# Where the first rounding of the attention output stands on ScalarE and VectorE, and which weight conversions stand behind it

## Chip, core and metric

The kernel runs on one core of one Trainium2 chip. The metric is the device time of one execution in microseconds (us). TensorE is called PE below, VectorE DVE, ScalarE ACT, GpSimd POOL, and SyncE, whose queue issues most transfers, SP.

## What is computed

An attention with a local window and block summaries feeds two gated or leaky feed-forward layers. Cut to what matters:

```python
k_sum = k.reshape(B, H, nb, 32, D).max(axis=3)      # 2 x 8 heads, 768 positions, D = 64
v_sum = v.reshape(B, H, nb, 32, D).mean(axis=3)
scores = concat([where(|i - j| < 16, q @ k.T / 8, -1e9), q @ k_sum.T / 8 + log(32)])
x = softmax(scores) @ concat([v, v_sum])            # 1536 tokens x 512
y = ((x @ w_a) * (x @ w_b)) @ w_out                 # 512 -> 1536 -> 512
h = y @ w_in; out = maximum(0.01 * h, h) @ w_out2   # 512 -> 2048 -> 512
```

## The kernel before

The attention is worked off in pairs of (head pair, 256 positions). For each pair PE turns q, multiplies the scores (line 670, `ps_t<-kts,qt`), DVE adds the mask and finds the extreme (line 684), ACT takes the exponential (line 690), DVE normalizes it (lines 699 to 701, in `normal`), PE turns the result (line 711), ACT copies it (line 715) and PE multiplies it with the values (line 725, in `pv`). Four such pairs give the first 512 tokens of x, one 128-row slice `x_0` to `x_3` for each pair.

The feed-forward products run in three passes of float32r matmuls: each operand is split into a rounded high part and a remainder. For x this is done at the end of `pv`: ACT rounds (line 735), DVE subtracts (line 736). A product is high x high, high x low, low x high (`mm3`).

The weights are stored as 64-bit words and are converted piece by piece (`convert`): SP loads a piece of 512 KB into `wst` (three buffers); DVE takes the low word (line 388), ACT the high word (line 394, `wc<-wst`), DVE clamps (400), shifts (403) and joins (409), ACT rounds the high part into `wsp` (416) and DVE subtracts the low part (419). `wc` has two buffers, so a third piece's line 394 waits until the first piece's line 419 is done. The pieces come in the order a0, b0, a1, b1, a2, ... While the attention runs, the first four weights a0, b0, a1, b1 are multiplied with each slice of x as it appears, into four banks `ps_a`, `ps_b`, `ps_c` (two of these).

A list of operations with planned places (`ops`) is sorted and recorded; `tick(2)` puts two steps of conversion behind most products. A scheduler then decides the order on each engine; `tc.issue_after(x)` keeps what is inside behind x. `line` is a chain that the first pairs' DVE work follows (`behind`).

The values for later pairs lie in two tiles, `vw0` (`vw_99`) and `vw1` (`vw_100`), with the block means added by a copy on POOL (line 224, `put_sums`). The second batch's block sums are made by loading a quarter of the values with SP (line 176, into `vb0` = `vb_101`) and adding the other three quarters by accumulating transfers that POOL issues (line 178), each of which waits until the one before has landed. Each SP transfer uses one of eight completion semaphores in turn and waits for the transfer eight places ahead of it.

Of the kernel before, what the change touches and what calls it, by code (L numbers as in the profile page):

```python
# [21 lines left out]
def kernel(  # L22
# [12 lines left out]
    nc = tc.nc  # L35
# [54 lines left out]
    cnt = {"at": 0, "q": 0, "conv": 0, "st": 0, "load": 0, "credit": 0.0, "bg": 0.0}  # L90
    late = {}

    def at_bank():
        cnt["at"] += 1
        return bank(at_banks[cnt["at"] % len(at_banks)])
# [12 lines left out]
    def runs(p):  # L108

        (b, hp, g), y = p  # L110
        if y == (b, hp, g + 1):
            return [(0, b, hp, g, 2)]
        return [(j, *x, 1) for j, x in enumerate(p)]
# [19 lines left out]
    bg, vb_done = [], [None, None]  # L133

    pace = {"micro": 0.0, "bg": 3, "after": None}
# [95 lines left out]
    LOAD, SIDE, PRODUCT = range(3)  # L231
    PER = 8
    PV = 13
# [111 lines left out]
    def need(key):  # L345
        return 2 if key[0] == "s" else 1

    def by_dma(key):
        return key[0] == "o" and key[1] >= M1 or key[0] == "p" and key[1] < M2
# [4 lines left out]
    def stage():  # L354
        key = loads[cnt["st"]]
        cnt["st"] += 1
        nm, f = key
        t = wst_p.tile([P, 1024], I32, tag="wst", name="wst")
        if nm in "op":
            src = {"o": w_o, "p": w_o2}[nm][P * f : P * (f + 1), :]  # L360
            nc.sync.dma_start(out=t, in_=src)
        else:
            src = {"a": w_a, "b": w_b, "i": w_i}[nm][:, 2 * P * f : 2 * P * (f + 1)]
            nc.sync.dma_start(
                out=t.rearrange("p (k f) -> p k f", k=KT),
                in_=src.rearrange("(k p) f -> p k f", p=P),
            )
        staged[key] = t

    def convert():  # L370

        i = cnt["conv"]
        key = pieces[i]
        while cnt["st"] < min(load_no[key] + 3, len(loads)):
            stage()
        cnt["conv"] += 1
        assert room[0] >= need(key), key
        room[0] -= need(key)
        if key[0] == "s":
            combine(key)  # L380
            return
        ww = staged.pop(key).rearrange("p (f two) -> p f two", two=2)
        lo_w, hi_w = ww[:, :, 0], ww[:, :, 1]
        t = {}

        def low():
            t["r"] = wcv_p.tile([P, 512], I32, tag="wr", name="wr")
            nc.vector.tensor_scalar(
                out=t["r"], in0=lo_w.bitcast(U32), scalar1=2.0**-29, scalar2=7.0,
                op0=ALU.mult, op1=ALU.min,  # L390
            )
            t["c"] = wcv_p.tile([P, 512], I32, tag="wc", name="wc")
            with tc.issue_after(pace["turned"].ins):
                nc.scalar.activation(  # L394
                    out=t["c"].bitcast(F32), in_=hi_w.bitcast(F32), func=AF.Abs, scale=2.0**-112
                )

        def clamp():
            c = t["c"].bitcast(F32)
            nc.vector.tensor_scalar(out=c, in0=c, scalar1=F_MAX, scalar2=None, op0=ALU.min)  # L400

        def shift():
            nc.vector.scalar_tensor_tensor(  # L403
                out=t["c"], in0=t["c"], scalar=3, in1=t["r"],
                op0=ALU.logical_shift_left, op1=ALU.bitwise_or,
            )

        def join():
            nc.vector.scalar_tensor_tensor(  # L409
                out=t["c"], in0=hi_w, scalar=SIGN, in1=t["c"],  # L410
                op0=ALU.bitwise_and, op1=ALU.bitwise_or,
            )

        def high():
            t["w"] = wsp_p.tile([P, 2, 512], F32R, tag="wsp", name="wsp")
            t["high"] = nc.scalar.copy(out=t["w"][:, 0], in_=t["c"].bitcast(F32))  # L416

        def rest_of():
            nc.vector.tensor_tensor(  # L419
                out=t["w"][:, 1], in0=t["c"].bitcast(F32), in1=t["w"][:, 0].bitcast(F32),  # L420
                op=ALU.subtract,
            )
            w_of[key] = t["w"]
            kept[key] = t["c"].bitcast(F32)

        def negative():
            t["n"] = wcv_p.tile([P, 512], F32, tag="wr", name="neg")
            nc.scalar.activation(
                out=t["n"], in_=t["w"][:, 0].bitcast(F32), func=AF.Copy, scale=-1.0
            )  # L430
            nc.gpsimd.dma_start(out=t["n"], in_=t["c"].bitcast(F32), accum_op=ALU.add)

        def low_of(after=None):
            with tc.issue_after(after.ins) if after is not None else nullcontext():
                nc.scalar.copy(out=t["w"][:, 1], in_=t["n"])
            w_of[key] = t["w"]

        bg.extend([low, clamp, shift, join, high])
        if lag:
            lows = lag.pop()  # L440
            bg.append(lambda: lows(t["high"]))
        bg.append(negative if by_dma(key) else rest_of)
        if by_dma(key):
            lag.append(low_of)

    def combine(key):
        x, y = pairs_of[key]
        c = kept.pop(x), kept.pop(y)
        t = {}

        def sub(o, x, y, op=ALU.subtract):
            at = lambda z: c[z[0]][:, z[1] * HB : (z[1] + 1) * HB]
            nc.vector.tensor_tensor(out=at(o), in0=at(x), in1=at(y), op=op)

        def high(j):
            t[j] = wsp_p.tile([P, 2, 512], F32R, tag="wsp", name="wsp")
            nc.scalar.copy(out=t[j][:, 0], in_=c[j])

        def rest_of(j):
            nc.vector.tensor_tensor(  # L460
                out=t[j][:, 1], in0=c[j], in1=t[j][:, 0].bitcast(F32), op=ALU.subtract
            )
            if j == 0:
                w_of[key] = t

        bg.extend([
            lambda: sub((1, 1), (1, 0), (1, 1), ALU.add),
            lambda: sub((1, 0), (0, 0), (1, 0)),
            lambda: high(1),
            lambda: sub((0, 0), (1, 1), (0, 0)),  # L470
            lambda: sub((0, 1), (0, 1), (0, 0)),
            lambda: high(0),
            lambda: rest_of(1),
            lambda: rest_of(0),
        ])
# [161 lines left out]
    st, placed, line = {}, [], []  # L637

    def in_line(ins):
        line.append(ins.ins)  # L640

    def behind(on):
        return tc.issue_after(line[-1]) if on else nullcontext()
# [51 lines left out]

    def normal(i, j):
        pm, sm = st["pm", i, j]
        with behind(i == 0):
            nc.vector.tensor_scalar_add(sm, sm, 1.0e-9)
        nc.vector.reciprocal(out=sm, in_=sm)  # L700
        done = nc.vector.tensor_tensor(
            out=pm, in0=pm, in1=sm.unsqueeze(2).to_broadcast([P, G, P]), op=ALU.mult
        )
        if i < 2:
            in_line(done)
# [12 lines left out]
    def pv(i, p):  # L718
        vw = vw_of.pop(i)
        ps = at_bank()  # L720
        for j in range(2):
            pt = st.pop(("pt", i, j))
            for w in range(G):
                for c in range(2):
                    st["out"] = nc.tensor.matmul(  # L725
                        out=ps[c * D : (c + 1) * D, j * GT + w * W : j * GT + (w + 1) * W],
                        lhsT=vw[:, j * G + w, c, :],
                        rhs=pt[:, w, c * W : (c + 1) * W],
                        start=True, stop=True,
                    )  # L730
        for j, b, hp, g, n in runs(p):
            c, t0 = divmod(b * S + g * GT, T)
            src = ps[:, j * GT : (j + n) * GT]
            x = x_tile(c, hp)[:, :, t0 : t0 + n * GT]
            nc.scalar.copy(out=x[:, 0], in_=src)  # L735
            nc.vector.tensor_tensor(
                out=x[:, 1], in0=src, in1=x[:, 0].bitcast(F32), op=ALU.subtract
            )


    def mm3(ps, w, x, first, last):
        for j, (a, b) in enumerate(((0, 0), (0, 1), (1, 0))):
# [38 lines left out]
    def first_weights(key, tag):  # L781
        ab0[key] = weights(key), bank(tag)
# [5 lines left out]
    N_FIRST = 5  # L788
    n_first = len(pairs[0])
    end = PER * (n_first - 1) + PV  # L790
    ops = attention_ops()
# [2 lines left out]
    ops.append((2.5, LOAD, lambda: [stage() for _ in range(3)], 0))  # L794
    firsts = ((("a", 0), "a"), (("b", 0), "b"), (("a", 1), "c0"), (("b", 1), "c1"))
    for i, x in enumerate(firsts):
        ops.append((PV, LOAD, lambda x=x: first_weights(*x), 0))
    ops.sort(key=lambda o: o[:2])
    rest = []
    for o in ops:  # L800
        if o[0] <= end or o[3] < n_first:
            o[2]()
            if o[1] == PRODUCT and o[0] >= PER+0.5 and (bg or cnt["conv"] < N_FIRST):
                tick(2)
        else:
            rest.append(o)
# [492 lines left out]
```

## Time and profile before

| | us |
|---|---|
| median of 3 runs | 637.85 |
| lowest, highest of the 3 | 636.07, 638.39 |
| the profiled execution | 635.28 |
| its span in the trace | 633.4 |

The profiled execution is 1.88 us longer than its span, and 2.57 us shorter than the median. Busy time in the profile: PE 611.6 us (97%), DVE 485.4 (77%), ACT 317.9 (50%), POOL 55.7 (9%). A row of the time line gives start, busy time, engine, source line and operation, output and inputs with their shapes, a count, and in brackets the engine's idle time before it and what ended that.

### The profile page before, as it was taken

Reading aid. Unit: us, or ns where it says so; the run is one execution under the profiler, and the core shown is the slowest. Engines: PE = TensorE matmul, PEld = TensorE weight load, DVE = VectorE, ACT = ScalarE, POOL = GpSimd, SP = SyncE. Lnnn points to the kernel's source line nnn. Section 1 sums busy time; section 2 is a strip of 40 time slices with the busy share of each in tenths; the row PEclk is TensorE's granted clock in tenths of the full one; section 3 lists DMA queues with packets and bytes.
Section 4 is the critical chain, followed back from the end, with each engine's and each line's share of the span. In section 5 each row is a group of like instructions: output and inputs, shape, how many; then the busy total and the mean of one; then the engine's idle time right before and its main releaser. Section 6 shows DMA issues by size and latency. Waiting matters only on the chain.

```text
span 633.4 us, 9456 instructions
## 1 busy us (share of the span) xinstructions
PE 611.6 (97%) x3344; PEld 498.5 (79%) x3344; DVE 485.4 (77%) x1070; ACT 317.9 (50%) x707; POOL 55.7 (9%) x101
## 2 busy tenths in 40 slices
PE   6589999999999999999999999999999999999997
PEld 4467777777888888888888888877888888888886
DVE  4996987853996869986889999687588576885552
ACT  5677885752545425434453648475463434443320
POOL 5224010000000001202120102000000000000000
PEclk9899999999999999999999999999999999999999
DMA  8989757620124503736593327323133013030013
GB/s 200 257 208 199 160 116 177 191 72 24 45 71 145 136 15 94 139 120 146 142 222 102 89 80 166 95 64 109 35 99 100 14 54 99 1 99 1 0 68 132
DMA packets 81006, 67.85 MB, mean 107 GB/s; under 512 B 47360, under 2 KB 67840, under 8 KB 80960
## 3 DMA queue, kind: packets, MB, share of 16 engines
q1 hardware_dynamic: 75808, 57.95, 31.7%
q0 software_dynamic: 5152, 9.31, 8.8%
q8 instruction: 26, 0.43, 0.3%
q14 instruction: 20, 0.16, 0.1%
HBM read 52.82 MB, written 10.49 MB: 100 GB/s over the span
## 4 chain that ended last, share of the span: by engine, by line
PE 80%; DVE 5%; DMA 5%; ACT 4%; issue 3%; SPq 1%; POOL 1%; POOLq 0%; DVEq 0%; ACTq 0%
PE ps_t L743 34%; PE ps_c L743 17%; PE ps_a L743 12%; PE ps_b L743 11%; PE ps_t L670 2%; DMA wst<-in_moe_w_out_dram 2%; PE ps_t L725 1%; PE ps_t L711 1%; ACT pm L690 1%; DMA neg<-wc 1%; DMA wst<-in_moe_w_a_dram 1%; DVE wc L403 1%; DMA q<-in_q_dram 1%; DVE wc L409 1%; SPq L209 1%
## 5 line engine op out<-in xcount | busy, mean ns | idle before, releaser
L743 PE MATMUL ps_c<-wsp,hs 128*128 128x512 f32 x288 | 75.1, 390 | 1.4 <-ACT acc L860 1.0
L743 PE MATMUL ps_t<-wsp,hs 128*128 128x512 f32 x288 | 74.5, 389 | 0.0
L743 PE MATMUL ps_t<-ys,wsp 128*128 128x512 f32 x270 | 68.2, 389 | 0.0
L394 ACT ACTIVATE wc<-wst 128x512 f32<-128x512 f32 x68 | 45.3, 673 | 45.2 <-DVE wsp L419 17.8
L743 PEld LDWEIGHTS ps_c<-wsp,hs 128*128 128x128 f32 x288 | 53.9, 188 | 13.3 <-ACT acc L860 1.4
L871 DVE TENSOR_TENSOR hs<-h,hs 128x512 fp32r<-128x512 f32 x72 | 49.3, 687 | 18.6 <-ACT hs L870 18.3
L743 PEld LDWEIGHTS ps_t<-wsp,hs 128*128 128x128 f32 x288 | 54.1, 188 | 11.2
L743 PEld LDWEIGHTS ps_t<-ys,wsp 128*128 128x128 f32 x270 | 50.7, 188 | 10.5
L870 ACT CAST hs<-h 128x512 fp32r<-128x512 f32 x72 | 44.5, 621 | 26.0 <-DVE h L1134 18.4
L416 ACT CAST wsp<-wc 128x512 fp32r<-128x512 f32 x68 | 41.8, 620 | 30.6 <-DVE wc L409 30.6
L743 PE MATMUL ps_a<-x,wsp 128*128 128x512 f32 x186 | 51.2, 403 | 4.5 <-ACT x L735 4.1
L743 PE MATMUL ps_t<-x,wsp 128*128 128x512 f32 x222 | 53.2, 389 | 0.0
L743 PE MATMUL ps_b<-x,wsp 128*128 128x512 f32 x192 | 51.7, 398 | 0.0
L1086 DVE TENSOR_TENSOR h<-ps_t,h 128x512 f32<-128x512 f32 x56 | 37.6, 687 | 17.0 <-PE ps_t L743 16.7
L1022 ACT ACTIVATE h<-h 128x512 f32<-128x512 f32 x32 | 20.2, 632 | 57.5 <-DVE h L1086 57.4
L743 PEld LDWEIGHTS ps_t<-x,wsp 128*128 128x128 f32 x222 | 41.7, 188 | 8.6
L403 DVE SCALAR_TENSOR_TENSOR wc<-wc,wr 128x512 int32<-128x512 int32 x68 | 46.5, 686 | 0.7
L409 DVE SCALAR_TENSOR_TENSOR wc<-wst,wc 128x512 int32<-128x512 int32 x68 | 46.6, 686 | 0.6
L743 PEld LDWEIGHTS ps_a<-x,wsp 128*128 128x128 f32 x186 | 33.9, 188 | 13.4 <-ACT x L735 4.6
L419 DVE TENSOR_TENSOR wsp<-wc,wsp 128x512 fp32r<-128x512 f32 x56 | 38.7, 697 | 5.8 <-ACT wsp L416 5.8
L743 PE MATMUL ps_t<-hs,wsp 128*128 128x512 f32 x144 | 42.7, 389 | 0.0
L690 ACT ACTIVATE pm<-pm,nb 128x128 f32<-128x128 f32 x96 | 37.5, 393 | 10.1 <-DVE nb L684 10.0
(129 smaller groups left out, 1098.1 us busy)
## 6 DMA issues: line engine op xcount, KB each, us to landing
wst<-in_moe_w_out_dram SPq DMA_DIRECT2D x28, 512.0 KB, 3.4
wst<-in_moe_w_in_dram SPq DMA_DIRECT2D x16, 512.0 KB, 3.8
wst<-in_moe_w_a_dram SPq DMA_DIRECT2D x12, 512.0 KB, 4.8
wst<-in_moe_w_b_dram SPq DMA_DIRECT2D x12, 512.0 KB, 4.0
y<-acc POOLq DMA_DIRECT2D x16, 256.0 KB, 6.1
y<-acc SPq DMA_DIRECT2D x12, 256.0 KB, 2.3
neg<-wc POOLq DMA_DIRECT2D x12, 256.0 KB, 3.5
acc<-y SPq DMA_DIRECT2D x12, 256.0 KB, 3.1
```

The costliest lines, as they stand in the source:

```text
L394: nc.scalar.activation(out=t["c"].bitcast(F32), in_=hi_w.bitcast(F32), func=AF.Abs, scale=2.0**-112)
L403: nc.vector.scalar_tensor_tensor(out=t["c"], in0=t["c"], scalar=3, in1=t["r"], op0=ALU.logical_shift_left, op1=ALU.bitwise_or,)
L409: nc.vector.scalar_tensor_tensor(out=t["c"], in0=hi_w, scalar=SIGN, in1=t["c"], op0=ALU.bitwise_and, op1=ALU.bitwise_or,)
L416: t["high"] = nc.scalar.copy(out=t["w"][:, 0], in_=t["c"].bitcast(F32))
L419: nc.vector.tensor_tensor(out=t["w"][:, 1], in0=t["c"].bitcast(F32), in1=t["w"][:, 0].bitcast(F32), op=ALU.subtract,)
L670: nc.tensor.matmul(out=ps[h, w, :], lhsT=qt[h, w * W : (w + 1) * W], rhs=kts[h, (g * G + w) * SC : (g * G + w) * SC + P], start=True, stop ...
L690: nc.scalar.activation(out=pm[:, w, :], in_=pm[:, w, :], func=AF.Exp, scale=-1.0, bias=nb[:, w : w + 1], accum_out=sm[:, w : w + 1],)
L743: nc.tensor.matmul(out=ps, lhsT=w(a), rhs=x(b), start=first and j == 0, stop=last and j == 2)
L870: pace["split"] = nc.scalar.copy(out=t[:, 0], in_=src)
L871: nc.vector.tensor_tensor(out=t[:, 1], in0=src, in1=t[:, 0].bitcast(F32), op=ALU.subtract)
L1022: nc.scalar.activation(out=h, in_=src, func=AF.Prelu, alpha=0.01)
L1086: nc.vector.tensor_tensor(out=out, in0=ps, in1=u, op=ALU.add)
```

## The change

Four edits, all in the first part of the program:

- the high word's step of every weight but the first (line 394) may not stand ahead of the first pair's x rounding on ACT;
- the second half of the second pair's normalizing (`normal(1, 1)`) stands behind the first pair's x subtraction on DVE;
- only the first weight (a0) is asked for at the place PV, the three others half a step later;
- up to PV, conversion steps are handed out between products only for one weight and no longer for five.

```diff
-            with tc.issue_after(pace["turned"].ins):
+            with tc.issue_after(pace["turned"].ins if i < 1 else pace["first x"].ins):
                 nc.scalar.activation(
                     out=t["c"].bitcast(F32), in_=hi_w.bitcast(F32), func=AF.Abs, scale=2.0**-112
...
-        with behind(i == 0):
+        after = st["low x"].ins if (i, j) == (1, 1) else line[-1]
+        with tc.issue_after(after) if i == 0 or (i, j) == (1, 1) else nullcontext():
             nc.vector.tensor_scalar_add(sm, sm, 1.0e-9)
...
-            nc.scalar.copy(out=x[:, 0], in_=src)
-            nc.vector.tensor_tensor(
+            hi = nc.scalar.copy(out=x[:, 0], in_=src)
+            lo = nc.vector.tensor_tensor(
                 out=x[:, 1], in0=src, in1=x[:, 0].bitcast(F32), op=ALU.subtract
             )
-
+            if i == 0:
+                pace["first x"], st["low x"] = hi, lo
...
-        ops.append((PV, LOAD, lambda x=x: first_weights(*x), 0))
+        ops.append((PV if i < 1 else PV + 0.5, LOAD, lambda x=x: first_weights(*x), 0))
...
-            if o[1] == PRODUCT and o[0] >= PER+0.5 and (bg or cnt["conv"] < N_FIRST):
+            n_now = 1 if o[0] < PV else N_FIRST
+            if o[1] == PRODUCT and o[0] >= PER+0.5 and (bg or cnt["conv"] < n_now):
                 tick(2)
```

No instruction of the computation is added or removed; the order on all five engines moves in the first 130 us or so of the program, and behind that it is the same. Three places matter below. On ACT, where the first pair's product with the values is rounded (`x_0`), the program before has:

```order
23 L394 ACTIVATE wc<-wst 128x512
24 L690 ACTIVATE pm,sm<-pm,nb 128x128
25 L394 ACTIVATE wc<-wst 128x512
26 L690 ACTIVATE pm,sm<-pm,nb 128x128 x2
27 L715 COPY pt<-ps_t_420 128x512
28 L690 ACTIVATE pm,sm<-pm,nb 128x128 x4
29 L416 CAST wsp<-wc 128x512
30 L394 ACTIVATE wc<-wst 128x512
31 L735 CAST x_0_507<-ps_t_490 128x512
32 L416 CAST wsp<-wc 128x512
```

And the changed one, at the same place:

```order
23 L394 ACTIVATE wc<-wst 128x512
24 L690 ACTIVATE pm,sm<-pm,nb 128x128 x3
25 L716 COPY pt<-ps_t_420 128x512
26 L690 ACTIVATE pm,sm<-pm,nb 128x128 x4
27 L416 CAST wsp<-wc 128x512
28 L736 CAST x_0_468<-ps_t_451 128x512
29 L394 ACTIVATE wc<-wst 128x512 x2
```

The steps of b0 and a1 (the second and third line 394) have moved behind the rounding of x.

On SP, from the load of the fourth weight (b1, the first `wst` row in both) on, before:

```order
24 L364 DMA wst<-in_moe_w_b_dram 128x4x256
25 L209 DMA vw_99<-in_v_dram 48x64
26 L209 DMA vw_99<-in_v_dram 64x7x64
27 L364 DMA wst<-in_moe_w_a_dram 128x4x256
28 L209 DMA vw_99<-in_v_dram 64x7x64
29 L209 DMA vw_99<-in_v_dram 32x8x64 x2
30 L156 DMA q<-in_q_dram 128x2x64 x4
31 L176 DMA vb_101<-in_v_dram 96x512
```

And in the changed program:

```order
23 L364 DMA wst<-in_moe_w_b_dram 128x4x256
24 L209 DMA vw_99<-in_v_dram 48x64 x2
25 L209 DMA vw_99<-in_v_dram 64x7x64 x2
26 L209 DMA vw_99<-in_v_dram 32x8x64 x2
27 L156 DMA q<-in_q_dram 128x2x64 x4
28 L176 DMA vb_101<-in_v_dram 96x512
29 L364 DMA wst<-in_moe_w_a_dram 128x4x256
```

The load of the fifth weight (a2) has moved behind the four q loads and the load of `vb_101`.

On POOL, where the block means are put into the value tiles for the third and fourth pair (`vw_99`, `vw_100`), before:

```order
51 L630 COPY kts_94<-ks_98 128x12x24
52 L178 DMA vb_101<-in_v_dram 96x512 x2
53 L224 COPY vw_99<-vs 24x1024
54 L224 COPY vw_100<-vs 24x1024
55 L178 DMA vb_101<-in_v_dram 96x512
```

And after:

```order
51 L630 COPY kts_94<-ks_98 128x12x24
52 L178 DMA vb_101<-in_v_dram 96x512 x3
53 L224 COPY vw_99<-vs 24x1024
54 L224 COPY vw_100<-vs 24x1024
55 L178 DMA vb_103<-in_v_dram 96x512
```

The third accumulating transfer into `vb_101` now stands ahead of the two copies.

## Rows read from the trace of the kernel before

**Rows 1.** The page's part 1: busy time, share of the span, instructions of each engine.
```profile
PE 611.6 (97%) x3344; PEld 498.5 (79%) x3344; DVE 485.4 (77%) x1070; ACT 317.9 (50%) x707; POOL 55.7 (9%) x101
```

**Rows 2.** Windows: stretch, length, busy time by engine (instructions), granted clock, DMA share, GB/s.
```profile
24.00:28.00 4.00, 0.36 (x2) 0.34 (x2) 4.00 (x13) 2.68 (x8) 0.00 (x0) 0.94 0.82 222
28.00:31.00 3.00, 3.00 (x20) 2.38 (x21) 3.00 (x7) 1.59 (x6) 0.00 (x0) 0.52 1.13 282
...
64.00:100.00 36.00, 35.56 (x376) 28.24 (x376) 31.09 (x124) 27.80 (x100) 4.37 (x7) 1.00 0.65 144
100.00:140.00 40.00, 39.70 (x308) 30.87 (x306) 29.28 (x95) 25.69 (x76) 2.05 (x3) 1.00 0.55 150
```

**Rows 3.** Time line of PE, 23 to 28 and 47 to 60 us.
```profile
23.15 0.87 PE L612 MATMUL ps_t<-ident,k 128*128 128x128 f32 x6
27.67 0.80 PE L743 MATMUL ps_a<-x,wsp 128*128 128x512 f32 x1 [3.64 <-ACT x L735]
...
47.29 1.15 PE L725 MATMUL ps_t<-pt,vw 128*64 128x64 f32 x32
...
50.19 0.41 PE L649 MATMUL ps_t<-ident,q 128*128 128x128 f32 x2 [0.36 <-DMA q<-in_q_dram]
...
50.79 0.48 PE L743 MATMUL ps_a<-x,wsp 128*128 128x512 f32 x1
...
54.46 1.08 PE L743 MATMUL ps_c<-x,wsp 128*128 128x512 f32 x4
...
59.21 0.50 PE L743 MATMUL ps_a<-x,wsp 128*128 128x512 f32 x1 [0.46 <-ACT x L735]
```

**Rows 4.** Time line of ACT, around the first x.
```profile
24.72 0.62 ACT L416 CAST wsp<-wc 128x512 fp32r<-128x512 f32 x1 [0.20 <-DVE wc L409]
26.47 0.68 ACT L394 ACTIVATE wc<-wst 128x512 f32<-128x512 f32 x1 [1.13 <-DVE wsp L419]
27.05 0.57 ACT L735 CAST x<-ps_t 128x512 fp32r<-128x512 f32 x1
```

**Rows 5.** Time line of DVE, 33 to 46 us.
```profile
33.03 0.43 DVE L388 TENSOR_SCALAR wr<-wst 128x512 int32<-128x512 uint32 x1 [1.07 <-DMA wst<-in_moe_w_b_dram]
33.80 0.43 DVE L400 TENSOR_SCALAR wc<-wc 128x512 f32<-128x512 f32 x1 [0.34 <-ACT wc L394]
34.14 0.28 DVE L684 CUSTOM_DVE_ANT_0 pm<-ps_t,negm_first 128x128 f32<-128x128 f32 x1
...
45.09 0.28 DVE L684 CUSTOM_DVE_ANT_0 pm<-ps_t,negm_first 128x128 f32<-128x128 f32 x1
```

**Rows 6.** Time line of SP's queue, 28 to 36 us.
```profile
28.67 1.33 SPq L364 DMA_DIRECT2D wst<-in_moe_w_a_dram  x1
...
35.47 0.34 SPq L176 DMA_DIRECT2D vb<-in_v_dram  x1
```

**Rows 7.** DMA issues: size, us from issue to landing (q at 33.8, vb at 35.5).
```profile
q<-in_q_dram SPq DMA_DIRECT2D x2, 64.0 KB, 3.3
...
vb<-in_v_dram SPq DMA_DIRECT2D x1, 192.0 KB, 4.3
```

**Rows 8.** The `wst` tile, 10 to 62 us: all weight loads, issue to landing.
```profile
DMA to landing us min/median/max: 4.9/5.9/6.8
```

**Rows 9.** Time line of POOL, 40 to 52 us.
```profile
40.08 0.96 POOL L178 DMA_DIRECT2D vb<-in_v_dram  x1 [7.83 <-DMA vb<-in_v_dram]
44.92 0.81 POOL L178 DMA_DIRECT2D vb<-in_v_dram  x1 [3.88 <-DMA vb<-in_v_dram]
45.77 2.47 POOL L224 COPY vw<-vs 24x1024 f32<-24x1024 f32 x2
50.43 1.61 POOL L178 DMA_DIRECT2D vb<-in_v_dram  x2 [2.19 <-DMA vb<-in_v_dram]
```

**Rows 10.** Lines 224 and 178 by source: duration in ns, least/median/most.
```profile
L224 POOL COPY vw<-vs x4: 1029/1133/1497, 19.3 to 46.7; 24x1024 f32<-24x1024 f32 x4
L178 POOL DMA_DIRECT2D vb<-in_v_dram x6: 792/898/1097, 40.1 to 61.8; - x6
```

## The prediction

> **What bounds the kernel now.** The page's first part comes first: PE is busy for 97% of the span [rows 1]. The windows then show where the other 3% lie. From 64 to 100 us PE is busy 35.56 of 36 us, from 100 to 140 us 39.70 of 40 [rows 2]. So behind 64 us the time is PE's own work, and an edit pays only if PE has the same work behind it sooner at about 64 us. In front of that PE waits: the one large hole is from 24.0 us, where the turning of the keys ends (23.15 and 0.87), to 27.67, where the first product with a weight starts, 3.64 us that ended with ACT's rounding of x [rows 3]. Behind the hole the granted clock is 0.52 from 28 to 31 us, that is nearly all of the stretch at 1.2 GHz [rows 2]. DVE is busy for the whole of 24 to 31 us [rows 2], so the other engines aren't free in the hole.
>
> Three later places are to be kept in view: the multiplication of the third pair with its values at 47.29, the first product with the third slice of x at 50.79, and with the fourth at 59.21 [rows 3].
>
> **The change, step by step.** *First x.* ACT rounds x at 27.05, behind a1's line 394, which waited 1.13 us for DVE to release `wc` [rows 4]. In the new order the rounding follows a0's rounding directly, which ends at 24.72 + 0.62 = 25.3. The product can begin some 0.57 later, at 25.9, against 27.67: a gain of 1.8 us at this place. The 3.64 us hole shrinks to under 2, and if that also spares the half clock, another 24 to 31 us term goes: 3 us at 0.52 do the work of 1.56, and 4 us at 0.94 cost 0.24, so at most 1.4 + 0.2 = 1.6 us. Together 3.4 us is the most that the front can give.
>
> *What PE does with it.* Little. b0, a1 and b1 are now converted behind x; each must go through the same six steps on a DVE that was already full. PE has work from 26 us on, but its next large pieces hang on the third pair's scores, which DVE takes at 34.14, and before that comes line 388 of b1, which waits for its load until 33.03 [rows 5]. That load keeps its place within one row of SP's queue, and the transfers ahead of it are the same, so it lands at about 33 again. What falls away is the clamp (33.80, after a 0.34 us wait) between line 388 and the scores [rows 5]: they start at about 33.4, 0.7 us sooner. That is all of the 1.8 us which is left by then.
>
> *The load of a2.* It was issued at 28.67 [rows 6]; now it stands behind four q loads and `vb_101`, and must also wait for b0's `wst` buffer. I put its issue at 35, from the 35.47 at which the `vb` load was issued [rows 6], and its landing at 40 with the shortest weight load of 4.9 us [rows 8]. a2's line 388 stands on DVE ahead of a1's and b1's remaining steps and of the second x subtraction. DVE would come to it at some 38, so it waits up to 2 us, and the fourth pair's scores at 45.09 [rows 5] come by up to 1 us later, not sooner. Least cost nothing, if the load lands by 38. I take the late end, but it costs the sum nothing as long as the next term is larger.
>
> *POOL's queue.* This is the term that counts. The third pair's values need the copy of line 224. Before, it followed the second accumulating transfer: 44.92, then 45.77 [rows 9], and with 1.03 to 1.13 us for a copy [rows 10] it was done at 46.8 to 46.9, half a microsecond ahead of the 47.29 at which PE needed it [rows 3]. Now the third transfer stands ahead, and that one waits until the second has landed. The steps: the SP load of `vb_101` was issued at 35.47, the time at which a2 had landed (28.67 + 6.8) [rows 6, 8]. With a2 gone from there I put it at 34.2, and its landing at 37.5, by the 3.3 us of the q loads just before it [rows 7]; the late end is 35.47 + 4.3 = 39.8, as before [rows 6, 7]. The first accumulating transfer follows 0.3 us later (40.08 behind 39.8) [rows 7, 9], so at 37.8. From the first to the second took 4.84 us (40.08 to 44.92), from the second to the third 5.51 (44.92 to 50.43) [rows 9]. That gives 37.8 + 4.84 + 4.84 = 47.5, or 48.2 with the longer step; I take 47.8. Issuing costs 0.85 (44.92 to 45.77) [rows 9], the copy 1.05 [rows 10]: done at 49.7. Ends: 49.4 and, with the late `vb` load and the longer step, 40.08 + 10.35 + 1.9 = 52.3. PE reaches this product at about 47.3, so it waits 2.4 us that it did not wait before.
>
> One price in this sum is disputed. The six issues of line 178 took 0.79 to 1.10 us [rows 10]. The Trainium skill, "SBUF — State Buffer", section "SBUF: two separate sides", says that GpSimd can't write the descriptors of its transfers while VectorE runs an instruction in a two-port mode, and gives about 0.6 us for one alone and 3.1 us for one overlapped. By that page the third issue could cost up to 3.1 us where I take 0.85, and the sum would be 2.25 us worse; no issue in this trace was stretched like that, so I stay with the row.
>
> *Behind the wait.* Two things change the distance to the third x. Four products of `ps_c` (1.08 us for four at 54.46, some 0.9 when they follow each other) [rows 3] stood ahead of the wait and now stand behind the first half of it; on the other side the 0.36 us wait for q at 50.19 [rows 3] goes, since q is no longer queued behind the load of a3. So the third x's product is at about 50.79 + 2.4 + 0.9 - 0.4 = 53.7. From there to 64 us PE gives some back: the 0.46 us before the fourth x at 59.21 [rows 3] and one group of four turnings that are now done earlier (0.4). What is left at 64 us is about 2.0. Of that the short waits behind 64 us (0.44 up to 100 us and 0.30 up to 140) [rows 2] can take in perhaps half. **Sum: +1.6 us.** On the profiled execution that is 635.28 + 1.6 = 636.9; on the median, which is 2.57 above it, 637.85 + 1.6 = 639.4. I forecast the median.
>
> **The rivals.** *Faster.* The front's gain holds: PE stays fed from 26 us on, the clock doesn't fall, and POOL's copy is done when PE gets there. That is -1.8 - 1.6 = -3.4, 634.4. It decides at the copy: the `vb` load would have to land 2.4 us before my 37.5, at 35.1. Against it stands that DVE is full in 24 to 31 us and that the same load of b1 ends its wait at 33.
>
> *Slower by the clock.* PE would now sit idle for 2.4 us at 47. The hole of 3.64 us that the trace has was followed by the half clock [rows 2, 3]. If it falls again, 1.4 to 1.6 us are lost, and the sum is +3.1: 641.0. The Trainium skill, "TensorE: Matmul & The Clock Gate", section "The HAM clock gate", also has the clock at 1.2 GHz after idling; whether this hole is enough no row here says.
>
> *Slower by a late copy.* If the `vb` load lands as late as before, the copy ends at 52.3 and not at 49.7: +1.6 + 2.6 = +4.2, 642.0. For it speaks that the transfers are 82 to 113% of capacity in 24 to 31 us [rows 2].
>
> *Nothing.* The third accumulating transfer comes through before PE asks, because PE itself is late from a2's wait; and what the front gains is used up at b1's load. Then the time is the old one, 637.9.
>
> **How the numbers follow.** Chances: forecast 0.50 (by itself 637 to 641), nothing 0.15, clock 0.12, late copy 0.13, faster 0.10. Half a per cent, 3.2 us, is about what a measurement of this kernel can tell from no change: under 634.7 is faster, over 641.0 slower. Slower takes half of the clock case, three quarters of the late copy and a tail of the forecast: 0.20. Faster takes most of its case: 0.09. The rest is 0.71. For eight in ten the range reaches into both: from 635.3, so that the faster case is left out, to 642.8, which leaves out the late copy together with a fallen clock.
>
> **What would show it.** In the profile of the changed kernel: x rounded on ACT at 25 to 26 us; the third pair's scores on DVE at about 33.4; DVE waiting for a `wst` load at line 388 near 38 to 40; three line 178 issues at about 37.8, 42.6 and 47.8 with the copy behind the last; PE idle for some 2.4 us before line 726 with POOL's copy as its releaser; the product with the third x at about 53.7. I am wrong if PE has no wait there, if the fourth x is reached before 59.2, or if the windows behind 64 us show new idle time on PE.

## The result, and the profile after

Over 4 runs each the changed kernel takes 644.59 us at the median (642.3 to 646.67), the kernel before 637.03. The ratio is 1.0116, with a 95% interval of 1.0074 to 1.0159: the change makes the kernel 7.6 us slower. That is above the top of the forecast range, 642.8. The profiled execution of the changed kernel took 646.67 us, the longest of its four, and that of before 635.28, so the two traces differ by 11.4 us, more than the medians do. (Of all executions in this document a single one, in e11 below, took 1686.2 us; it is left out of that run's ratio.)

Page, part 1, of the changed kernel (span and PE's busy time):

```profile
span 644.4 us, 9457 instructions
...
PE 616.9 (96%) x3344; PEld 501.7 (78%) x3344; DVE 486.0 (75%) x1070; ACT 317.8 (49%) x707; POOL 55.9 (9%) x101
```

The same 3344 matmuls are busy 5.3 us longer than in [rows 1]. No work was added, and the mean granted clock is 0.986 where it was 0.996, so this is time at the lower clock. PE's idle time is span less busy time: 633.4 - 611.6 = 21.8 us before, 644.4 - 616.9 = 27.5 us now, 5.7 us more. The two make up the 11.0 us between the spans.

Windows of the changed kernel (columns as in rows 2):

```profile
24.00:28.00 4.00, 1.48 (x13) 0.96 (x13) 3.97 (x14) 3.93 (x13) 0.00 (x0) 1.00 0.80 186
28.00:32.00 4.00, 3.29 (x41) 2.54 (x38) 3.87 (x9) 1.28 (x6) 0.60 (x1) 1.00 1.13 266
32.00:36.00 4.00, 1.50 (x14) 0.86 (x13) 1.96 (x10) 1.81 (x7) 0.15 (x1) 0.93 0.73 124
36.00:42.00 6.00, 5.33 (x50) 3.95 (x46) 4.05 (x15) 4.42 (x17) 0.96 (x1) 0.50 0.86 241
...
54.00:58.00 4.00, 4.00 (x32) 3.06 (x28) 0.72 (x1) 0.73 (x2) 1.57 (x3) 0.50 1.04 232
64.00:100.00 36.00, 34.46 (x353) 27.01 (x352) 30.37 (x112) 27.37 (x96) 6.72 (x11) 1.00 0.61 135
100.00:140.00 40.00, 39.94 (x309) 31.25 (x308) 32.42 (x111) 26.75 (x85) 2.01 (x3) 1.00 0.53 146
```

The window of 32 to 36 us in the kernel before:

```profile
32.00:36.00 4.00, 4.00 (x44) 2.89 (x43) 2.63 (x11) 2.71 (x10) 0.25 (x1) 1.00 1.11 237
```

The low clock of 28 to 31 us [rows 2] is gone, and two new stretches at 0.50, which is the 1.2 GHz level, have come, at 36 to 42 and at 54 to 58 us. From 24 to 36 us PE is idle for 5.7 us (12 less 1.48, 3.29 and 1.50). DVE is busy for 1.96 us of 32 to 36, where it was 2.63 before. From 64 to 100 us PE is idle for 1.54 us, where [rows 2] have 0.44; behind that it is nearly full. Most of the loss is made in front: counted from the end of the program, the matmul that stood at 72 us comes 9.5 us later than before, and those of 114 to 310 us come 9.86 us later. The last 1.1 us come near 330 us, at a place that the last section takes up.

Time line of PE:

```profile
26.67 0.63 PE L712 MATMUL ps_t<-ident,pm 128*128 128x128 f32 x4 [2.27 <-DVE pm L702]
27.05 0.48 PE L745 MATMUL ps_a<-x,wsp 128*128 128x512 f32 x1
...
35.57 1.12 PE L726 MATMUL ps_t<-pt,vw 128*64 128x64 f32 x16 [2.27 <-DVE nb L684]
...
53.25 1.12 PE L726 MATMUL ps_t<-pt,vw 128*64 128x64 f32 x16 [3.41 <-POOL vw L224]
54.30 2.08 PE L745 MATMUL ps_c<-x,wsp 128*128 128x512 f32 x4
...
60.17 0.48 PE L745 MATMUL ps_a<-x,wsp 128*128 128x512 f32 x1
69.10 0.50 PE L745 MATMUL ps_a<-x,wsp 128*128 128x512 f32 x1 [0.78 <-ACT x L736]
```

Against [rows 3] the third pair's multiplication with its values has gone from 47.29 to 53.25 us, the product with the third x from 50.79 to 60.17, and with the fourth from 59.21 to 69.10. The wait of 3.41 us ends with POOL's copy. Behind it four products take 2.08 us, where 1.08 is the time at the full clock [rows 3].

Time line of POOL:

```profile
40.09 0.96 POOL L178 DMA_DIRECT2D vb<-in_v_dram  x1 [7.94 <-DMA vb<-in_v_dram]
45.31 0.81 POOL L178 DMA_DIRECT2D vb<-in_v_dram  x1 [4.25 <-DMA vb<-in_v_dram]
51.09 0.79 POOL L178 DMA_DIRECT2D vb<-in_v_dram  x1 [4.98 <-ACT wc L394]
51.93 2.25 POOL L224 COPY vw<-vs 24x1024 f32<-24x1024 f32 x2
```

The third issue waits for the second transfer to land (the row names ACT, which is not what the instruction reads), and the copy stands behind it, as the new order on POOL has it.

Time line of ACT:

```profile
25.94 0.58 ACT L736 CAST x<-ps_t 128x512 fp32r<-128x512 f32 x1
```

Time line of DVE:

```profile
34.04 0.43 DVE L388 TENSOR_SCALAR wr<-wst 128x512 int32<-128x512 uint32 x1 [2.18 <-DMA wst<-in_moe_w_b_dram]
34.38 0.28 DVE L684 CUSTOM_DVE_ANT_0 pm<-ps_t,negm_first 128x128 f32<-128x128 f32 x1
...
41.12 0.43 DVE L388 TENSOR_SCALAR wr<-wst 128x512 int32<-128x512 uint32 x1 [1.95 <-DMA wst<-in_moe_w_a_dram]
...
47.57 0.28 DVE L684 CUSTOM_DVE_ANT_0 pm<-ps_t,negm_first 128x128 f32<-128x128 f32 x1
```

Time line of SP's queue:

```profile
26.37 0.44 SPq L364 DMA_DIRECT2D wst<-in_moe_w_b_dram  x1
26.91 4.57 SPq L209 DMA_DIRECT2D vw<-in_v_dram  x6
31.52 3.93 SPq L156 DMA_DIRECT2D q<-in_q_dram  x4
35.50 0.46 SPq L176 DMA_DIRECT2D vb<-in_v_dram  x1
36.07 0.37 SPq L364 DMA_DIRECT2D wst<-in_moe_w_a_dram  x1
```

The load of a2 is issued at 36.07, where [rows 6] have 28.67. x is rounded 1.1 us sooner than in [rows 4]. DVE waits for the loads of b1 (2.18 us) and of a2 (1.95 us), 4.1 us together where [rows 5] have 1.07 at this line. The fourth pair's scores come at 47.57 and not at 45.09 [rows 5].

### The profile page after: what moved, and what is told of

Same layout as the page of the kernel before. It is cut to its first block, busy times and chain, and to the rows that moved or that the text cites. A ratio compares the mean times of both kernels' runs of the same rounds, so it can differ in the third digit from the quotient of the medians.

```text
span 644.4 us, 9457 instructions
## 1 busy us (share of the span) xinstructions
PE 616.9 (96%) x3344; PEld 501.7 (78%) x3344; DVE 486.0 (75%) x1070; ACT 317.8 (49%) x707; POOL 55.9 (9%) x101
## 4 chain that ended last, share of the span: by engine, by line
PE 79%; DVE 8%; DMA 6%; issue 4%; ACT 2%; POOL 1%; SPq 0%; POOLq 0%; ACTq 0%; DVEq 0%
PE ps_t L745 33%; PE ps_c L745 18%; PE ps_a L745 11%; PE ps_b L745 11%; PE ps_t L670 2%; DMA neg<-wc 2%; PE ps_t L726 2%; PE ps_t L712 1%; ACT pm L690 1%; DMA k<-in_k_dram 1%; DVE h L1089 1%; DMA vw<-in_v_dram 1%; DMA wst<-in_moe_w_out_dram 1%; DMA wst<-in_moe_w_a_dram 1%; DVE wc L403 1%
## 5 line engine op out<-in xcount | busy, mean ns | idle before, releaser
L388 DVE TENSOR_SCALAR wr<-wst 128x512 int32<-128x512 uint32 x68 | 29.2, 431 | 19.5 <-ACT wsp L435 8.8
L690 ACT ACTIVATE pm<-pm,nb 128x128 f32<-128x128 f32 x96 | 37.5, 395 | 11.4 <-DVE nb L684 11.4
L745 PE MATMUL ps_c<-hs,wsp 128*128 128x512 f32 x144 | 42.4, 390 | 0.3 <-DVE acc L866 0.3
```

The costliest lines, as they stand in the source:

```text
L388: nc.vector.tensor_scalar(out=t["r"], in0=lo_w.bitcast(U32), scalar1=2.0**-29, scalar2=7.0, op0=ALU.mult, op1=ALU.min,)
L690: nc.scalar.activation(out=pm[:, w, :], in_=pm[:, w, :], func=AF.Exp, scale=-1.0, bias=nb[:, w : w + 1], accum_out=sm[:, w : w + 1],)
L745: nc.tensor.matmul(out=ps, lhsT=w(a), rhs=x(b), start=first and j == 0, stop=last and j == 2)
```

## Experiments

Two things in the new order could each make the loss. **Theory A**: on POOL the third accumulating transfer stands ahead of the copies. **Theory B**: in the front, x stands ahead of the conversions, and with them the loads of b1 and a2 come late. **Theory C** says that half of the loss is the clock that falls behind a wait. **Theory D** came after the first eight runs: all of it hangs on the place of b0's conversion alone. The runs stand in four groups, and each is compared with runs of the kernel before beside it on the same chip; where times are set against it, the difference of the two medians is meant. In kernels with added lines the line numbers lie some lines higher.

**First group: e1 to e4** (kernel before 635.47 us, 21 runs).

*e1*, the changed kernel with POOL's old order (the order on PE, DVE and SP stays that of the changed kernel):

```diff
+                elif j == 3 and i == 0:
+                    held_back.append((t, src))
...
-            put(
+            done = put(
...
+        if i == 3:
+            t, src = held_back.pop()
+            with tc.issue_after(done.ins):
+                nc.gpsimd.dma_start(out=t, in_=src, accum_op=ALU.add)
```

> The changed kernel, but the third accumulating transfer into vb_101 stands on POOL behind the two copies of line 224 again, as before the change; all else is as in the changed kernel. Theory A (the order on POOL makes the loss: the late copy leaves PE idle for 3.4 us at 50 to 53 us, and the half clock behind it, four products in 2.08 us where 1.08 us is the full-clock time, takes about 3 us more): the copy ends at about 47 to 48 us, PE doesn't wait for POOL at line 726, the half clock of 53 to 59 us is gone, and the time falls by about 6.5 us, to 638. Theory B (the front makes the loss: x ahead of the conversions delays b1 and a2, DVE waits at line 388, and the half clock falls at 36 to 42 us): the POOL wait goes, PE is late anyway, and the time falls by under 1.5 us, to 643 or more.

Measured: 640.67 us, ratio 1.0074 (1.0052 to 1.0097), 5.2 us over the kernel before. Time line of PE in e1:

```profile
49.27 0.69 PE L734 MATMUL ps_t<-pt,vw 128*64 128x64 f32 x16
...
55.14 0.50 PE L753 MATMUL ps_a<-x,wsp 128*128 128x512 f32 x1 [1.20 <-ACT x L744]
...
63.76 0.50 PE L753 MATMUL ps_a<-x,wsp 128*128 128x512 f32 x1 [0.78 <-ACT x L744]
```

POOL's wait and the clock's fall behind it are gone, as theory A has it (from 50 to 60 us the granted clock is 1.00). But PE comes to 49.27 two microseconds late, and the fourth x is 4.55 us late. Most of the loss is still there, without POOL.

*e2*, the kernel before with POOL's new order alone (ACT, DVE and SP keep theirs, and on PE one matmul moves within its group):

```diff
-                    nc.gpsimd.dma_start(out=t, in_=src, accum_op=ALU.add)
+                    tied["acc", i, j] = nc.gpsimd.dma_start(out=t, in_=src, accum_op=ALU.add)
...
-            put(
...
+            with tc.issue_after(tied["acc", 0, 3].ins) if i in (2, 3) else nullcontext():
+                put(
```

> The kernel before, with one thing of the change alone: the two copies of line 224 for the third and the fourth pair stand on POOL behind the third accumulating transfer. Theory A: the copy ends at about 52.3 us and not at 46.9, PE, which wants it at 47.3, is idle for about 5 us, the half clock follows, and the time rises by 5 to 7 us, to 642.5 to 645. Theory B: PE waits there but makes it good from work that stands ready behind, and the time stays within 1.5 us of 637.

Measured: 641.63 us, ratio 1.0089 (1.0058 to 1.0119), 6.2 us over. Time line of PE in e2:

```profile
51.36 1.98 PE L726 MATMUL ps_t<-pt,vw 128*64 128x64 f32 x32 [4.44 <-POOL vw L225]
```

From 50 to 54 us the granted clock is 0.50. Theory A holds for this part. So either part costs 5 to 6 us alone, and both together cost 7 to 8.

*e3*, the changed kernel with PE's wait for POOL filled:

```diff
+        for _ in range(28 if i == 2 else 0):
+            nc.tensor.matmul(out=ps[:, 0:P], lhsT=ident, rhs=ident, start=True, stop=True)
```

> The changed kernel with work added: 28 throwaway products of 128x128 (the identity with itself, into the bank that the third pair's multiplication with its values overwrites), so that PE has something to do while it waits for POOL's copy. Theory C (half of the loss is the clock, which falls because PE idled): the granted clock stays near 1 from 50 to 60 us, and the time falls by 2.5 to 3.5 us, to 641 to 642, although the copy comes no sooner. If the clock isn't part of the loss: the same time as the changed kernel, or more by what of the added work doesn't fit into the wait.

Measured: 645.09 us, ratio 1.014 (1.0107 to 1.0172). The clock stays at 1.00 from 50 us on, but the 28 products take 6.7 us and put the multiplication off to 56.5 us. The dose was twice too large, so this run doesn't tell what the clock is worth; e6 repeats it with half.

*e4*, the changed kernel without its first edit:

```diff
-            with tc.issue_after(pace["turned"].ins if i < 1 else pace["first x"].ins):
+            with tc.issue_after(pace["turned"].ins):
```

> The changed kernel without its first edit: the conversions of b0, a1 and b1 aren't tied behind the first x, the other edits stay. POOL then has its copies ahead of the third accumulating transfer, and a2's load stands where it stood before. Theories A and B both give the old time, 637 within 1 us; if it is slower by over 2 us, one of the other edits (the second x subtraction ahead of line 702, or the count of ticks) has a cost that neither theory has.

Measured: 638.07 us, ratio 1.0039 (1.0016 to 1.0062), 2.6 us over: a remainder that neither theory had. Time line of PE in e4:

```profile
50.10 1.15 PE L726 MATMUL ps_t<-pt,vw 128*64 128x64 f32 x32 [1.82 <-POOL vw L224]
```

POOL's copy is late here too, though it has its old place: the second accumulating transfer was issued only at 48.17, and from 50 to 54 us the clock is 0.68. e10 takes this up.

**Second group: e5 to e8** (kernel before 636.45 us, 20 runs).

*e5* is the changed kernel, unaltered.

> The changed kernel, unaltered, so that its time stands in one comparison with the three runs beside it. All theories: 1.010 to 1.014 of the kernel before, 6.5 to 9 us over it, with PE's wait of about 3.4 us for POOL's copy at 50 us and the half clock at 36 to 42 and at 53 to 59 us.

Measured: 643.71 us, ratio 1.0106 (1.0077 to 1.0135), 7.3 us over. The wait for POOL is 3.40 us.

*e6* is e3 with 14 throwaway products in place of 28.

> The changed kernel with 14 throwaway products of 128x128 in the wait for POOL's copy, in place of 28. In the run before, 28 of them took 6.7 us, against a wait of 3.4, so that the added work put off by 3.2 us what the steady clock gave back; 14 take about 3.3 us and fit. Theory C (the half clock behind the wait costs about 3 us): the granted clock stays near 1 from 50 to 60 us, and the time is 2.5 to 3.5 us under the changed kernel of this comparison. If the clock costs nothing: within 1 us of it.

Measured: 642.51 us, ratio 1.0095 (1.0071 to 1.0119), 1.2 us under e5, which the intervals don't separate. Window of 50 to 60 us in e5 (columns as in rows 2):

```profile
50.00:60.00 10.00, 7.87 (x79) 6.18 (x81) 4.50 (x15) 5.06 (x20) 5.79 (x7) 0.83 0.86 212
```

The same window in e6:

```profile
50.00:60.00 10.00, 10.00 (x109) 8.58 (x110) 6.38 (x27) 6.82 (x23) 5.62 (x7) 1.00 0.90 219
```

The wait is filled and the clock doesn't fall. From the start of the copies to the product with the third x it is 7.30 us in e5 (50.43 to 57.73) and 5.42 us in e6 (51.85 to 57.27): in these two traces the steady clock is worth at most some 1.9 us, not theory C's 3. It isn't the clock alone: with the added products the order moves too. In e6 four products of `ps_c` stand between the throwaway products, ahead of the multiplication with the values; in e5 they follow its first half.

*e7* is e1 with 8 such products ahead of the second pair's multiplication with its values (the loop of e3 with `8 if i == 1`).

> The changed kernel with POOL's copies ahead of the third accumulating transfer, as in the first run, and with 8 throwaway products of 128x128 ahead of the second pair's multiplication with its values, where PE waits 1.9 us at 33 to 35 us. Theory B in the form that the front's price is the half clock at 36 to 42 us, which the wait brings: the clock stays near 1 there, and the time falls by 2.5 to 3.5 us against the first run, to some 2 us over the kernel before. If the front's price is the late conversions themselves (DVE held by the loads of b1 and a2): under 1 us less than the first run, that is 4 to 6 us over the kernel before.

Measured: 642.41 us, ratio 1.0083 (1.0057 to 1.0109). The run missed its aim: the products stood in the bank that the waiting multiplication needs, waited with it and ran at 36.2 us, 3.75 us long at the low clock. e12 does it again in another bank.

*e8*, the kernel before with POOL's copies still earlier, ahead of the second transfer too (e1's edit with `j > 1`).

> The kernel before, with the second and the third accumulating transfer into vb_101 both behind the two copies of line 224 on POOL; nothing else moves. The copies can then start when ACT has written vs (42.4 us) and not at 45.8. If the copy behind the second transfer is near the edge (in the run without the first edit the second transfer began at 48.2 us and PE waited 1.8 us; in the profile of before it made it by half a microsecond): PE never waits for POOL at 47 us, and the median falls by up to 1.5 us, to 634 to 635.5. If the later transfers are then late for the sums behind them: slower by 1 to 2 us. Otherwise the same.

Measured: 637.02 us, ratio 1.0004 (0.9987 to 1.0021). PE doesn't wait for POOL in this trace, and nothing is gained: the kernel before has no such loss to give back.

**Third group: e9 to e11** (kernel before 636.21 us, 29 runs). If in the changed kernel b0's step alone is tied behind x and those of a1 and b1 are not, the order on all five engines comes out the same as in the changed kernel; if b0's is left free and the others are tied, it comes out nearly as in the kernel before: the same on SP, but on POOL the fourth pair's copy, and only that, stands behind the third transfer. Hence theory D, and *e9*:

```diff
-            with tc.issue_after(pace["turned"].ins if i < 1 else pace["first x"].ins):
+            with tc.issue_after(pace["turned"].ins if i < 2 else pace["first x"].ins):
```

> The changed kernel, but the conversion of b0, too, is left where it was; only those of a1 and b1 are tied behind the first x. On the engines' queues nearly the whole reordering is then gone: a2's load, the products of x0 and POOL's copies stand as before, and x is rounded ahead of line 394 of a1. Theory D (the loss comes from b0 alone, which stands ahead of everything else: products with b0 and a1 that filled PE from 28 to 36 us come late, and all later queues shift): the time is that of the kernel before, 636 within 1 us, or up to 1.5 us less, since x comes 1.1 us sooner. If the order of x and a1, or the second x subtraction ahead of line 702, is what costs: 2 us or more over the kernel before.

Measured: 636.48 us, ratio 1.0007 (0.9985 to 1.0028). Time line of PE in e9:

```profile
26.22 0.49 PE L745 MATMUL ps_a<-x,wsp 128*128 128x512 f32 x1 [1.50 <-ACT x L736]
...
60.47 0.50 PE L745 MATMUL ps_a<-x,wsp 128*128 128x512 f32 x1 [0.46 <-ACT x L736]
```

The whole loss is gone with this one figure. SP's order and the third pair's copy go back to their old places with b0, so e9 is to be read against e1, where the copy has its old place too and b0 stands behind x. The product with x begins 1.45 us sooner than in [rows 3], the thing that the change is about, and the fourth x comes no sooner than before.

*e10*, e4 with POOL's copies ahead of the second transfer too.

> The kernel of the fourth run (the changed kernel without its first edit), with the second and the third accumulating transfer behind POOL's copies; nothing else moves. That run was 0.39% over the kernel before, and its profile shows PE waiting 1.8 us for the copy at 50 us, with the half clock behind it. If that wait is its loss: no wait for POOL, and the time is back within 1 us of the kernel before. If the loss comes from the other edits elsewhere: it stays at 2 us or more.

Measured: 637.14 us, ratio 1.0008 (0.9986 to 1.003). PE doesn't wait for POOL any more. That the late copy was e4's remainder is likely; the intervals of e4 and e10 overlap a little.

*e11*, e9 and e8's edit together.

> The kernel of the run with b0 not moved, together with the second and the third accumulating transfer behind POOL's copies: the version that should beat both if either part gives anything. If x sooner by 1.1 us counts and no wait for POOL is left: 1 to 2 us under the kernel before. If PE's own work is all that counts behind 64 us: the same within 1 us.

Measured: 637.17 us, ratio 1.001 (0.999 to 1.0029). No version beats the kernel before. Windows of e11 (columns as in rows 2):

```profile
24.00:36.00 12.00, 7.02 (x60) 4.84 (x60) 10.51 (x31) 6.85 (x22) 0.75 (x1) 1.00 1.05 241
36.00:42.00 6.00, 4.89 (x50) 3.80 (x51) 6.00 (x20) 4.89 (x17) 1.12 (x1) 0.55 0.69 184
28.00:44.00 16.00, 12.72 (x112) 9.23 (x113) 14.51 (x45) 8.62 (x30) 1.88 (x2) 0.79 0.94 220
```

PE is idle for 5.0 us of 24 to 36 us here and the clock is low from 36 to 42, nearly as in the changed kernel, and yet nothing is lost. DVE, though, is full from 36 to 42.

**Fourth group: e12** (kernel before 635.59 us, 11 runs). It is e1 with the throwaway products behind the second product with b0:

```diff
+                for _ in range(8):
+                    with tc.issue_after(st["b0 product", 1].ins):
+                        nc.tensor.matmul(
+                            out=ab0["b", 1][1][:, 0:P], lhsT=ident, rhs=ident,
+                            start=True, stop=True,
+                        )
```

> As the run with the filled front, but the 8 throwaway products of 128x128 go into the bank of b1's product, which is free, right behind the first two products with b0. In that run they stood in the bank that the waiting multiplication needs, so that they waited with it and began at 36.2 us, behind the wait and not in it. Now they should run at 33.2 to 35.1 us. If the wait is what brings the half clock at 36 to 42 us: the clock stays near 1 there and the time falls by 2 to 3 us against the first run, to some 2 to 3 us over the kernel before. If the clock falls all the same, or its price is small: within 1 us of the first run, 4 to 6 us over the kernel before.

Measured: 639.79 us, ratio 1.0069 (1.005 to 1.0087), against 1.0074 of e1. Time line of PE in e12 (a throwaway product has two rows):

```profile
33.21 1.95 PE L803 MATMUL ps_c<-ident 128*128 128x128 f32 x16
...
42.00 0.51 PE L753 MATMUL ps_c<-x,wsp 128*128 128x512 f32 x1 [1.77 <-DVE wsp L427]
...
63.78 0.50 PE L753 MATMUL ps_a<-x,wsp 128*128 128x512 f32 x1 [0.74 <-ACT x L744]
```

Window of 36 to 42 us in e1:

```profile
36.00:42.00 6.00, 5.04 (x36) 3.84 (x37) 4.14 (x17) 4.33 (x16) 0.97 (x1) 0.50 0.81 233
```

The same window in e12:

```profile
36.00:42.00 6.00, 3.12 (x39) 2.07 (x36) 4.08 (x16) 4.25 (x17) 0.96 (x1) 1.00 0.94 258
```

This time the wait is filled and the clock stays at 1.00. PE gets through its work sooner, is then idle for half of the stretch, waits 1.77 us for DVE at its end, and comes to the fourth x at 63.78 us, where e1 without the filling came at 63.76. So the low clock of 36 to 42 us shows no price here. The limits are that the intervals of the two ratios leave room for some 2 us, and that the filling moves other instructions too (the load of b2 is issued at 36.93 us and not at 38.76).

What DVE does in 28 to 44 us goes with the loss. The window of this stretch in the kernel before (the third busy column is DVE's):

```profile
28.00:44.00 16.00, 13.87 (x123) 10.15 (x123) 14.59 (x43) 9.75 (x32) 1.72 (x2) 0.91 0.89 211
```

In e9:

```profile
28.00:44.00 16.00, 14.09 (x120) 10.50 (x121) 14.52 (x44) 9.21 (x30) 1.72 (x2) 0.81 0.90 211
```

In e1:

```profile
28.00:44.00 16.00, 12.06 (x109) 8.59 (x106) 12.30 (x40) 8.36 (x29) 1.72 (x2) 0.79 0.89 208
```

In the changed kernel:

```profile
28.00:44.00 16.00, 11.70 (x106) 8.44 (x103) 11.88 (x38) 8.18 (x28) 1.71 (x2) 0.79 0.91 208
```

DVE gets through 14.5 to 14.6 us of work where b0 has its old place, and 11.9 to 12.3 where it stands behind x. The 2.2 to 2.7 us that are missing lie in the waits at line 388, 4.1 us in the changed kernel against 1.07 before. All fourteen traces divide like this: 13.8 to 15.1 us in the seven with b0 at its old place (e11 with 14.51 among them), 10.7 to 12.6 in the seven with b0 behind x. Of the two waits, only the one for a2 divides them: 1.8 to 2.3 us in each of the latter seven, none in the former. The one for b1 is 0.6 to 2.3 us with b0 at its old place and 1.6 to 3.1 behind x; e8 loses nothing with 1.8.

## Why the prediction was wrong

The four cases side by side, as ratios to the kernel before of the same group:

| | b0 at its old place | b0 behind x |
|---|---|---|
| third pair's copy ahead of the third transfer | 1.0007 (e9) | 1.0074 (e1) |
| third transfer ahead of both copies | 1.0089 (e2) | 1.0106 (e5) |

e4 belongs in the first field too (1.0039), with a copy that was late for another reason.

**The step that failed** is the front: under "What PE does with it" the answer was "Little", with 0.7 us left of the gain, and a2's late load "costs the sum nothing as long as the next term is larger". Alone the front costs 5.2 us (e1), and that hangs on b0's step (e9). The step looked at when x is ready and not at what b0's step holds up. One way can be followed in the rows. a2 is loaded into the `wst` buffer that b0 leaves, and b0 reads it last in line 409. Time line of DVE in the kernel before, and behind the dots in the changed kernel:

```profile
26.35 0.68 DVE L409 SCALAR_TENSOR_TENSOR wc<-wst,wc 128x512 int32<-128x512 int32 x1
...
31.19 0.68 DVE L409 SCALAR_TENSOR_TENSOR wc<-wst,wc 128x512 int32<-128x512 int32 x1
```

a2's load, 7.4 us later on SP, then keeps DVE waiting. DVE, whose fullness was the argument that nothing could be gained, was itself held up by two loads. That this is the whole way is not shown: no run moves a2's load alone, and the 2.3 us that DVE lacks in e1 are about half of the 4.55 us by which the fourth x is late there. PE's idle time in front doesn't make the price by itself. Before, the products with b0 and with the first `ps_c` weight filled PE from 28 to 36 us; in the changed kernel they are not ready then, and PE is idle for 5.7 of the 12 us from 24 to 36. But in e11 it is idle for 5.0 of them, at the time of the kernel before.

**Point by point.** The rounding of x was put at 25 to 26 us and came at 25.94. The product behind it was put at 25.9 and came at 27.05, since on PE a turning stands ahead of it that waits for line 702 on DVE; the step took ACT's time for PE's. The third pair's scores were put at 33.4 and came at 34.38: b1's load, said to land "about 33 again", was issued no later (26.37, against 26.95 before) and yet took 7.6 us and not 6.1. On the queue six `vw` loads now follow directly behind it, where two stood. That these share its way is not borne out: the load took 7.2 us in e8, with the order before, and 5.7 in e3, with the changed one. The cause stays open. a2's wait was put at up to 2 us, and was 1.95; its price was put at nothing. In e1, with no wait for POOL to hide it, the fourth x comes 4.55 us later than in [rows 3]. One reading of the clock rows was too large as well: PE is busy for 0.36 us in 24 to 28 [rows 2], so the 0.94 there can't cost 0.2.

**POOL's term** was right in kind and too small: the sum took 1.6 us from it, and alone it costs 6.2 (e2), so that by size this step missed by nearly as much as the front. The three issues were put at 37.8, 42.6 and 47.8 us and came at 40.09, 45.31 and 51.09; PE's wait, put at 2.4 us, was 3.41. The `vb` load was to come sooner, "With a2 gone from there": it was issued at 35.50, as before, since the four q issues ahead of it took 3.93 us where they took 2.17. This is the rival of the late copy, and it had 0.13. POOL alone costs 6.2 us (e2), the front alone 5.2, and both 7.3, since they lie partly in one another: with the late front PE waits 3.4 us for the copy and not 4.4, and the 1.20 us ahead of the third x in e1 disappears in that wait. The other 2 us of the overlap are not told apart.

**The clock** was put at 1.4 to 1.6 us as a rival with 0.12. It was no case of its own but came with the waits. Its size was about right, in part by luck: it fell behind the wait, as priced, but also at 36 to 42 us, while the old stretch at 28 to 31 went. The mean granted clock of e5's six runs is 0.9890 and that of the 20 runs of before beside them 0.9914; at half speed in the slow stretches that is 2 x 0.0024 x 640 = 3.1 us more at the low level, worth at most 1.5 us. In the two profiled executions it is 5.3 us; one has more than its share of it. Theory C, half of the loss, isn't borne out: e6 got back 1.2 us, and this estimate is 1.5.

**The disputed price.** The issues of line 178 took 0.78 to 0.96 us again. The 3.1 us that the Trainium skill, "SBUF — State Buffer", section "SBUF: two separate sides", gives for an overlapped one were not seen, although DVE is busy at the second and the third; whether in a two-port mode, the profile doesn't say, so this is no proof against the page.

**The range.** Its top left out the late copy together with a fallen clock as if the two were independent. In all four traces in which PE waits 1.8 to 4.4 us for the copy with nothing put into the wait (the changed kernel, e2, e4, e5) the clock falls behind it. By the prediction's own prices both together give 642.0 + 1.6 = 643.6, 1.0 us under what was measured. And no case let the front lose. Of the three signs of being wrong one came true, "new idle time on PE" behind 64 us (1.54 against 0.44 us up to 100). The sign of the fourth x looked the wrong way: it named a time before 59.2, and the product comes at 69.10. In the other traces this one row goes roughly with the time: 59.21 before, 60.47 in e9, 60.48 in e11, 60.84 in e8, 62.07 in e10, 63.18 in e4, 63.76 in e1, 63.78 in e12, 64.67 in e2, 65.42 in e7, 65.44 in e6, 66.67 in e5, 67.77 in e3.

## What to carry to other kernels

When an instruction is moved ahead of others, price what is pushed back by all that hangs on it, not by how full its own engine is: here one weight conversion out of three carried a buffer, with it the place of a load, and with that a wait on DVE, whose work PE needed next. Where a wait falls away but nothing gets sooner some tens of microseconds on (e9, e12), the engine that waited was probably not the bound; look for the first row further on that moves. And rivals that share a cause, such as a late transfer, a wait and the clock behind it, belong into one case with the sum of their prices.

## What the runs showed of the hardware

The granted clock of one and the same kernel differs from run to run, with means of 0.988 to 0.997. Of the 20 runs of the kernel before in the second group, the five with a mean of 0.995 or more took 635.2 us on the mean, and the eight with 0.989 or less 637.3. A wait doesn't settle it: behind 2.27 us of waiting at 24.4 to 26.7 us in the changed kernel the clock stays at 1.00, and behind another 2.27 us at 33.3 to 35.6 it is 0.50.

One accumulating transfer of 256 KB near 330 us took 5.6 us from its issue to the copy on ACT that reads it in the profile of before (327.20 to 332.82), and 9.0 us in e3 (335.19 to 344.19), at the same place in the program. PE then waits 0.2 to 2.7 us behind it in every trace but that of before, e8 and e9 included, whose times are those of before; so this is no part of the change's loss, but 1.1 of the 11.0 us between the two spans lie there.

The load of b1 (512 KB) took 5.0 to 7.9 us from issue to landing in the fourteen traces, and neither end of that goes with one of the two orders on SP.
